# Three exchanges in the order in which a linear-attention and feed-forward kernel issues its loads

## The chip, the core and the metric

The kernel runs on one core of a Trainium2 chip. The core has a matrix engine (TensorE, PE in the profile; its weight loads are shown as PEld), two elementwise engines (VectorE, DVE; ScalarE, ACT), a general one (GpSimd, POOL) and SyncE (SP), which here does nothing but issue transfers between the chip's main memory and the core's SBUF. Each engine works through its own list of instructions in order and waits on semaphores for the others. The metric is the device time of one execution in microseconds; lower is better. A comparison goes by the median of several executions.

## What is computed

Causal linear attention with a decay per head, over 4 batches, 8 heads, 768 positions and head size 64, and behind it a feed-forward layer with a leaky ReLU. Inputs are q, k, v, the decay `lam`, and the weights `w_in` (512 x 2048) and `w_out` (2048 x 512). The weights arrive as float64.

```python
for b in range(nb):                                   # blocks of 64 positions
    qb, kb, vb = (q[:, :, sl], k[:, :, sl], v[:, :, sl])
    intra = np.einsum('bhic,bhjc->bhij', qb, kb) * Dmask[None]
    intra = np.einsum('bhij,bhjd->bhid', intra, vb)
    inter = np.einsum('bhid,bhde->bhie', qb * lam_pow[None], kv_state)
    out[:, :, sl] = intra + inter
    kb_dec = kb * rev_pow[None]
    kv_state = lam_block[None, :, None, None] * kv_state + np.einsum('bhsd,bhse->bhde', kb_dec, vb)
...
x = attn_out.transpose(0, 2, 1, 3).reshape(B * S, H * D)   # 3072 x 512
h = x @ w_in
g = np.maximum(0.01 * h, h)
return g @ w_out
```

## The kernel before

**Chunks.** The attention goes through 24 chunks of 128 positions (6 per batch), all 8 heads at once. For chunk c, `load_kq` loads k and q (two transfers each, L476) and `load_v` loads v (one transfer, L538). `transposes` turns k and q on TensorE (L560) into PSUM; copies on ACT or DVE (L541) bring them back as kT and qT, and L608 makes a scaled copy of qT. `scores` has two products: `kv`, the state update from k and v, and `go`, the scores from kT and qT (both L420). `outputs` has three: `own` (scores times v), and the halves `inter(0)` and `inter(1)` of the product of q with the states (L420). Between the two halves stands a tiny copy from PSUM, `seen_po` (L692), on ACT or DVE; `inter(1)` waits for it. L708, L716 and L734 then write the chunk's result as three parts xh, xl, xm, which keep float32 accuracy in the product with the weights. Up to chunk 7, q is loaded like k; from chunk 8 on it comes in small pieces of 32x8x32 (L523).

**Weights.** `w_in` is taken in 8 blocks p of 256 columns, each in two halves h. `to_float32` loads one half as float64 into one of three buffers raw0, raw1, raw2 (two transfers of 256 KB, L798), and builds a float32 of it: three steps on ACT (L810, L812, L814) and two on DVE (L816, L817). `parts` splits the block into a head wh (L823), wm (L826) and wl (L828). `up` multiplies a group of four chunks with one block (L864), and `down` the result with `w_out` (L930), with TensorE alone at work for the last half of the time.

**Order.** `Plan` holds every step as an operation with a number, an engine, what it reads and what it writes. The list `ORDER` (L266) fixes the order of the first 1296 entries by hand: pairs of an operation number and an engine, "DMA" being SP. An entry with a negative number stands for idle products that keep TensorE busy. What comes behind the list is ordered by a planner's costs. Each engine gets its operations in the order of the list; only the order among entries of the same engine matters. Semaphore waits follow from what each operation reads and writes. SP's line in the list is one queue: a transfer whose buffer is not free yet holds up every transfer behind it.

**The entries that the change touches,** all on SP:

| entry | what it loads | who needs it |
|---|---|---|
| 95 | first half of w_in block 1, into raw1, two transfers | steps 97 (L812), 96 (L810), 98 (L814) on ACT, 99 and 100 on DVE, then wh1 (107, L823 on ACT) |
| 50 | q of chunk 2, two transfers | transpose 53 (L560) |
| 74 | v of chunk 3, one transfer | `kv` of chunk 3 (81, L420) |
| 111 | q of chunk 4, two transfers, into the buffer of q of chunk 2 | transpose 114 (L560) |
| 355 | second half of w_in block 7, into raw2, two transfers | steps 356 (L810), 357 (L812), 358 (L814) on ACT, then wh7 |
| 275 | one small piece of the q of chunks 8 and 9 | DVE transposes (L532) |
| 303 | v of chunk 8, one transfer | `kv` of chunk 8 (310, L420) |

On ACT the order around them is 102 (L810), 103 (L812), 97 (L812), 104 (L814), 96 (L810), 98 (L814), 44 (L692, chunk 1), 54 (L541), 46 (L708), 107 (L823); operations 101 to 106 belong to the other half of block 1, which is loaded into raw0 just ahead of entry 95. Later it is 356, 357, 358, 309 (L692, chunk 7), 313 (L708). On DVE it is 106 (L817, second half), 55 (L541), 99 (L816), 100 (L817, first half).

## Time and profile before

| | |
|---|---|
| median of 3 executions | 607.43 us (606.27 to 608.04) |
| profiled execution | 606.49 us, of which 604.7 us from the first to the last instruction |
| TensorE | busy 595.9 us, 99% of the span, granted clock 1.0 |
| DVE, ACT, POOL | 49%, 35%, 12% |
| read from and written to main memory | 68.69 and 35.65 MB, 173 GB/s over the span |

Times in the profile are microseconds from the start of the span. A line names the kernel's line (L798), the engine, the operation, and what it writes and reads by the program's tile names; in brackets stands the idle time of the engine ahead of it and what ended that. SPq is SP's queue: there, start and length are those of the issue, not of the transfer. When a transfer lands is shown by the view of transfers, as the time from issue to landing. The tile `att` holds all of the attention's buffers, so k, q and v of most chunks are written to it; chunks 2 and 3 use `gs` and `raw` for some of theirs. Every product of 64x64 or 128x128 tiles in float32 shows as one or two matmuls.

### The profile page before, as it was taken

To read this page: it belongs to the slowest core of one execution; us is meant where nothing else is said; L and a number is where in the kernel's file an instruction comes from. 1 tells how busy PE (TensorE), PEld (TensorE's weight loads), DVE (VectorE), ACT (ScalarE), POOL (GpSimd) and SP (SyncE) were. 2 spreads that over 40 slices of the span, in tenths; PEclk is the share of its full clock that TensorE was granted. 3 is DMA by queue.
4 is the path that set the end of the run, shared out by engine and by line. 5 is a ranking of instruction groups with operands and counts; after the bars stand their busy time and mean duration, and the time that the engine had idled before them with its cause. 6 is when DMAs were issued, how large, how long until landed. Compare 5 with 4: busy or idle time off the path is not lost.

```text
span 604.7 us, 12740 instructions
## 1 busy us (share of the span) xinstructions
PE 595.9 (99%) x5362; PEld 492.0 (81%) x5362; DVE 294.4 (49%) x410; ACT 209.2 (35%) x323; POOL 70.0 (12%) x84
## 2 busy tenths in 40 slices
PE   8899999999999999999999999999999999999997
PEld 5788888888888888887888888888888888888886
DVE  6798754450554434244167755354353543534430
ACT  4686651212433433435334421222312313214111
POOL 2311232241322031140000000000000000000000
PEclk9999999999999999999999999999999999999999
DMA  9998887597788788664975823433333333423201
GB/s 208 226 266 224 224 241 199 88 258 188 214 227 210 224 241 232 183 203 181 327 258 184 302 105 128 151 99 134 116 116 128 118 126 122 125 102 124 85 1 69
DMA packets 150249, 105.18 MB, mean 174 GB/s; under 512 B 126128, under 2 KB 126896, under 8 KB 150192
## 3 DMA queue, kind: packets, MB, share of 16 engines
q1 hardware_dynamic: 148848, 104.03, 58.6%
q8 instruction: 42, 0.69, 0.5%
q10 hardware_dynamic: 1344, 0.33, 0.2%
q14 instruction: 15, 0.12, 0.1%
HBM read 68.69 MB, written 35.65 MB: 173 GB/s over the span
## 4 chain that ended last, share of the span: by engine, by line
PE 95%; DMA 2%; SPq 1%; issue 0%; ACT 0%; DVE 0%; DVEq 0%; ACTq 0%
PE b L864 32%; PE b L930 16%; PE pt L864 11%; PE psc L930 11%; PE po L930 11%; PE pt L930 5%; PE po L420 4%; PE psc L420 3%; DMA att<-in_v_dram 2%; DMA att<-in_q_dram 1%; PE b L560 0%; PE po L560 0%; SPq L798 0%; PE b L420 0%; PE b L359 0%
## 5 line engine op out<-in xcount | busy, mean ns | idle before, releaser
L912 DVE SCALAR_TENSOR_TENSOR xl<-att,xh 128x1024 fp32r<-128x1024 f32 x48 | 58.7, 1223 | 125.8 <-ACT xh L911 125.8
L911 ACT ACTIVATE xh<-att 128x1024 fp32r<-128x1024 f32 x48 | 50.9, 1061 | 147.5 <-PE po L930 73.0
L864 PE MATMUL b<-xl,wl 128*128 128x512 f32 (+1 forms) x292 | 77.1, 388 | 0.0
L864 PE MATMUL b<-xh,wh 128*128 128x512 f32 (+1 forms) x292 | 76.5, 389 | 0.6 <-ACT wh L823 0.6
L864 PE MATMUL b<-xm,wm 128*128 128x512 f32 (+1 forms) x292 | 76.0, 390 | 0.0
L891 ACT ACTIVATE gs<-b 128x512 f32<-128x512 f32 x72 | 42.1, 597 | 96.3 <-PE b L864 87.1
L864 PEld LDWEIGHTS b<-xh,wh 128*128 128x128 f32 x292 | 53.9, 188 | 11.8 <-ACT wh L823 0.7
L864 PEld LDWEIGHTS b<-xl,wl 128*128 128x128 f32 x292 | 54.1, 188 | 11.2
L864 PEld LDWEIGHTS b<-xm,wm 128*128 128x128 f32 x292 | 53.8, 188 | 11.2
L914 DVE SCALAR_TENSOR_TENSOR xm<-xl,xh 128x1024 fp32r<-128x1024 f32 x48 | 58.8, 1226 | 4.7
L930 PE MATMUL b<-wh,xh 128*128 128x512 f32 x144 | 56.0, 389 | 0.0
L930 PE MATMUL b<-wl,xl 128*128 128x512 f32 x144 | 56.0, 389 | 0.0
L930 PE MATMUL b<-wm,xm 128*128 128x512 f32 x144 | 56.0, 389 | 0.0
L663 POOL TENSOR_TENSOR att<-att 128x256 f32<-128x256 f32 x40 | 27.8, 694 | 113.9 <-DVE att L660 66.2
L930 PE MATMUL psc<-wm,xm 128*128 128x512 f32 (+1 forms) x100 | 38.2, 387 | 0.0
L930 PE MATMUL po<-wm,xm 128*128 128x512 f32 (+1 forms) x100 | 37.9, 384 | 0.0
L930 PE MATMUL psc<-wh,xh 128*128 128x512 f32 x96 | 37.3, 389 | 0.0
L930 PE MATMUL psc<-wl,xl 128*128 128x512 f32 x96 | 37.3, 389 | 0.0
L930 PE MATMUL po<-wh,xh 128*128 128x512 f32 x96 | 37.3, 389 | 0.0
L930 PE MATMUL po<-wl,xl 128*128 128x512 f32 x96 | 37.3, 389 | 0.0
L420 PEld LDWEIGHTS po<-att 64*64 64x64 f32 x1408 | 27.0, 134 | 10.5 <-issue 7.8
L420 PE MATMUL po<-att 64*64 64x64 f32 x1408 | 33.0, 222 | 1.7 <-issue 0.9
(106 smaller groups left out, 860.5 us busy)
## 6 DMA issues: line engine op xcount, KB each, us to landing
att<-g SPq DMA_DIRECT2D x48, 512.0 KB, 3.4
g<-gs SPq DMA_DIRECT2D x47, 512.0 KB, 3.6
raw<-in_moe_w_in_dram SPq DMA_DIRECT2D x32, 256.0 KB, 4.3
raw<-in_moe_w_out_dram SPq DMA_DIRECT2D x16, 512.0 KB, 4.6
out_dram<-gs SPq DMA_DIRECT2D x23, 256.0 KB, 2.1
att<-in_v_dram SPq DMA_DIRECT2D x22, 256.0 KB, 3.8
att<-in_k_dram SPq DMA_DIRECT2D x43, 128.0 KB, 3.9
wo<-w SPq DMA_DIRECT2D x8, 512.0 KB, 4.0
```

What stands on the lines that cost most here:

```text
L420: nc.tensor.matmul(dst[HALF[cols]], lhsT=lhsT[HALF[rows]], rhs=rhs[HALF[rows]], start=start, stop=True, skip_group_check=True)
L663: add("POOL", 0.62, lambda new=new, j=j: behind(("s", j), nc.gpsimd.tensor_tensor(state[(j + 1) % 4], new, _bc(lam_c, 2, D), op=ALU.mult)) ...
L864: nc.tensor.matmul(dst, lhsT=w[z][:, kk * 2 * P + f * P:kk * 2 * P + (f + 1) * P], rhs=x[z][:, kk, toks], start=start and kk == 0, stop=kk ...
L891: add("ACT", ns, lambda b=b, r=r: nc.scalar.activation(out=r(), in_=b(), func=AF.Prelu, bias=0.0, scale=1.0, alpha=0.01), [kb], [kg], rank ...
L911: add("ACT", 1.05, lambda: nc.scalar.activation(out=h, in_=graw[j], func=AF.Copy, bias=0.0, scale=NEAR), reads, wr("h"))
L912: add("DVE", 1.215, lambda: nc.vector.scalar_tensor_tensor(l, graw[j], 1.0, h.bitcast(F32), op0=ALU.mult, op1=ALU.subtract), reads + [f"rh ...
L914: add("DVE", 1.215, lambda: nc.vector.scalar_tensor_tensor(m, l.bitcast(F32), -S, h.bitcast(F32), op0=ALU.mult, op1=ALU.add), [f"rh{j}", f ...
L930: nc.tensor.matmul(to[:, cols], lhsT=ring[j][z][:, f * T + tb * P:f * T + (tb + 1) * P], rhs=W[pp][z][:, f * d_model:(f + 1) * d_model][:, ...
```

## The change

Three places of `ORDER` are changed. Only entries of SP change their order among themselves; the other entries are moved along in the text of the list, but keep their order on their engines.

1. q of chunk 2 (50) is issued ahead of the first half of w_in block 1 (95), which was ahead of it.
2. q of chunk 4 (111) is issued ahead of v of chunk 3 (74).
3. v of chunk 8 (303) is issued where the second half of w_in block 7 (355) was, ahead of one small q piece (275), and 355 where v of chunk 8 was, behind that piece.

```diff
-    ... (101, "DMA"), (95, "DMA"), (50, "DMA"), (20, "PE"), (49, "DMA"), (72, "DMA"), ...
+    ... (101, "DMA"), (50, "DMA"), (95, "DMA"), (20, "PE"), (49, "DMA"), (72, "DMA"), ...
...
-    ... (98, "ACT"), (44, "ACT"), (74, "DMA"), (41, "POOL"), ... (57, "DVE"), (111, "DMA"), (58, "PE"), ...
+    ... (98, "ACT"), (44, "ACT"), (111, "DMA"), (74, "DMA"), (41, "POOL"), ... (57, "DVE"), (58, "PE"), ...
...
-    ... (304, "DMA"), (355, "DMA"), (288, "ACT"), (275, "DMA"), (207, "POOL"), ... (293, "DVE"), (303, "DMA"), ...
+    ... (304, "DMA"), (303, "DMA"), (275, "DMA"), (355, "DMA"), (288, "ACT"), (207, "POOL"), ... (293, "DVE"), ...
```

## The prediction

> **What bounds the kernel now.** I read the page's first two lines, then the stretches from 30 us on, then TensorE's waits. The columns of the first fence are engine, busy time, share and instructions.

> ```profile
> span 604.7 us, 12740 instructions
> PE 595.9 (99%) x5362; PEld 492.0 (81%) x5362; DVE 294.4 (49%) x410; ACT 209.2 (35%) x323; POOL 70.0 (12%) x84
> ```

> By stretches (from:to, its length, busy time of PE, PEld, DVE, ACT, POOL, granted clock, DMA share, GB/s):

> ```profile
> 30.00:67.00 37.00, 36.98 (x613) 31.61 (x615) 31.42 (x49) 26.20 (x48) 7.88 (x11) 1.00 0.87 234
> 75.00:300.00 225.00, 225.00 (x2741) 185.91 (x2740) 92.28 (x176) 81.77 (x146) 52.01 (x56) 1.00 0.77 213
> 300.00:595.00 295.00, 295.00 (x1303) 244.35 (x1302) 140.93 (x122) 77.89 (x93) 0.00 (x0) 1.00 0.39 133
> ```

> From 75 to 595 us TensorE is never idle. So whatever the change wins or loses must be won or lost before 75 us, and from there it goes to the end one for one: nothing behind it can absorb a delay, and nothing can lengthen a gain. What there is to win stands in TensorE's waits (who waited for whom, total us, times, longest):

> ```profile
> PE po L420 <- issue: 0.9, 1, 0.9
> PE b L560 <- DMA att<-in_q_dram: 0.6, 1, 0.6
> PE b L864 <- ACT wh L823: 0.6, 1, 0.6
> PE psc L420 <- DMA att<-in_v_dram: 0.5, 1, 0.5
> ```

> The second is the transpose of q of chunk 4, the fourth the state product of chunk 8, which needs v8. The chain that ended last passes through the same two loads (start, length from issue to landing):

> ```profile
> 20.64 5.37 DMA att<-in_q_dram
> 64.17 3.54 DMA att<-in_v_dram
> ```

> q4's second half lands at 26.01, v8 at 67.71. Both would land earlier. The third wait, for the head wh1 of w_in block 1, is what the first exchange could lengthen.

> **The change part by part.** Nothing is added or removed. Every engine but SP keeps its order, and on SP the same loads are issued, so what is costed is when each load lands and who stands in line behind it.

> *Exchange 1, q2 ahead of the first half of w_in block 1 (entry 95).* SP's issues (start, length, operation):

> ```profile
> 7.12 2.49 SPq L798 DMA_DIRECT2D raw<-in_moe_w_in_dram  x4
> 9.19 0.43 SPq L798 DMA_DIRECT2D raw<-in_moe_w_in_dram  x1
> 9.66 0.98 SPq L476 DMA_DIRECT2D att<-in_q_dram  x2
> 10.14 0.51 SPq L476 DMA_DIRECT2D att<-in_q_dram  x1
> ```

> Landings of the pieces issued at 9.19, 9.66 and 10.14, in that order (the last column is us from issue):

> ```profile
> raw<-in_moe_w_in_dram SPq DMA_DIRECT2D x1, 256.0 KB, 4.4
> ...
> att<-in_q_dram SPq DMA_DIRECT2D x1, 128.0 KB, 5.8
> ...
> att<-in_q_dram SPq DMA_DIRECT2D x1, 128.0 KB, 5.7
> ```

> The load of w lands at 9.19 + 4.4 = 13.6, q2's halves at 15.4 and 15.8. The loads of this queue land in the order of issue, so in the new order w comes last of the four, and between 14.4 and 15.8: at the least 0.4 us for each q2 half (the distance of their own landings) after 13.6, at the most where the four together end now. I take 15.8: same queue, same bytes, same stretch of time. That is 2.2 us later. Now the line behind it. ACT and DVE (start, length, operation):

> ```profile
> 13.66 0.79 ACT L812 ACTIVATE low<-raw 128x512 uint16<-128x512 uint32 x1
> ...
> 14.30 0.76 ACT L814 ACTIVATE low<-raw 128x512 f16<-128x512 f32 x1
> 14.93 0.65 ACT L810 ACTIVATE w<-raw 128x512 f32<-128x512 f32 x1
> 15.47 0.79 ACT L814 ACTIVATE low<-raw 128x512 f16<-128x512 f32 x1
> 17.03 0.16 ACT L692 COPY att<-po 128x2 f32<-128x2 f32 x1 [0.77 <-PE po L420]
> ...
> 18.61 1.05 ACT L823 CAST wh<-w 128x1024 fp32r<-128x1024 f32 x1
> ...
> 15.32 0.68 DVE L817 CUSTOM_DVE_ANT_0 w<-w,low 128x1024 uint16<-128x1024 uint16 x1
> 16.61 0.69 DVE L541 COPY att<-b 128x512 f32<-128x512 f32 x1 [0.60 <-PE b L560]
> ...
> 17.77 0.69 DVE L817 CUSTOM_DVE_ANT_0 w<-w,low 128x1024 uint16<-128x1024 uint16 x1
> ```

> The L812 at 13.66 reads this load, and it stands in ACT's line ahead of an L814 that works on the other half (already landed), ahead of two more steps on w, and ahead of the L692 copy that lets TensorE go on with chunk 1. All of them move by 2.2: the L814 of 14.30 ends at 15.06 + 2.2 = 17.3; L692 starts at about 18.4 instead of 17.03. On DVE the first L817 needs that L814 and starts 0.26 behind it, at 17.5; the L541 copy behind it at 18.15; the second L817, 1.16 after the copy, at 19.3, and ends at 20.0. The cast of wh1 starts 0.15 behind it as now: 20.15, ends 21.2, against 19.66. The other way to it, L692, then TensorE's second half of chunk 1, then the copy xh, then the cast, gives about 19.85 and is not the last. So the product on wh1 is 1.5 us late. On the way to the transpose of q4 at 24.9 I let TensorE make good 0.2 (an estimate: waits for loads that do not move, each below the 0.15 us at which the view begins): +1.3.

> What q2 gains is worth nothing: its transpose starts right behind the 0.9 us of "issue" in the waits, in which TensorE waited for no load, and that stays. If that stall went, q2's landing would be the next to hold it, now early.

> *Exchange 2, q4 ahead of v3.*

> ```profile
> 19.48 0.43 SPq L538 DMA_DIRECT2D gs<-in_v_dram  x1
> 20.01 1.45 SPq L476 DMA_DIRECT2D att<-in_q_dram  x2
> ```

> q4 goes to the place of v3 and lands before the 26.01 of now, whatever v3 takes. TensorE comes to its transpose at 24.9 + 1.3 = 26.2, so the 0.6 wait is gone, and 0.1 more before its second half: -0.7. v3 takes the last place of the three and lands by 26.0 (where they end now); its first user starts at 26.9 now and at 27.5 then. q4's issue also waits for its buffer, until the transposes of q2 are done, and those are over by 16.6; v3 and v8 wait for no buffer, so nothing is held on SP by the new order. Balance of the two exchanges: 1.3 - 0.7 = +0.6. Without exchange 1 the second alone would give about -0.7.

> *Exchange 3, v8 ahead of the second half of w_in block 7 (entry 355).* Its two pieces go behind v8 and behind one small q piece:

> ```profile
> 61.46 2.19 SPq L798 DMA_DIRECT2D raw<-in_moe_w_in_dram  x2
> 61.96 1.69 SPq L798 DMA_DIRECT2D raw<-in_moe_w_in_dram  x1
> 63.70 0.42 SPq L523 DMA_DIRECT2D att<-in_q_dram  x1
> 64.17 0.45 SPq L538 DMA_DIRECT2D att<-in_v_dram  x1
> ```

> Landing of the piece issued at 61.96:

> ```profile
> raw<-in_moe_w_in_dram SPq DMA_DIRECT2D x1, 256.0 KB, 4.3
> ```

> So w is complete at 66.3 and v8 at 67.7. ACT and TensorE behind them:

> ```profile
> 66.37 0.70 ACT L810 ACTIVATE w<-raw 128x512 f32<-128x512 f32 x1 [2.77 <-DMA raw<-in_moe_w_in_dram]
> ...
> 68.24 0.14 ACT L692 COPY att<-po 128x2 f32<-128x2 f32 x1
> ...
> 67.84 1.16 PE L420 MATMUL psc<-att 64*64 64x64 f32 x64 [0.53 <-DMA att<-in_v_dram]
> 68.79 0.44 PE L420 MATMUL po<-att 64*64 64x64 f32 x16
> ```

> With v8 early TensorE's 67.84 becomes 67.3, and its 68.79 (the second half of chunk 7) 68.3. But that one needs the L692 copy, and the copy stands in ACT's line behind three steps on w: it starts 1.87 after the L810, and TensorE can follow 0.2 later. The new landing of w is between 66.3 (v8 fits into the pauses) and 67.7 (the end of the three loads now). I take 67.3, 66.3 plus v8's 256 KB at the 0.4 us that 128 KB of q took above, and a little: the L810 at 67.4, the copy at 69.25, TensorE at 69.45 instead of 68.79: +0.65. The ends are 66.3: 68.45, -0.35, and 67.7: 69.85, +1.05. The wait is not removed, it goes from v8 to w, by way of ACT. The stream here is started by TensorE's own progress, so the +0.6 of before is added. What w itself is for (head wh7) is used by TensorE only near 81 us and does not matter.

> *The fetch of instructions.* The landings above are not even: w at 13.6, then q2 only at 15.4. In that stretch the program's instructions are also fetched. The page's row for it, and the count in the one microsecond from 12.5 us (queue, kind, number, MB, share):

> ```profile
> q8 instruction: 42, 0.69, 0.5%
> ...
> q8 instruction: 1, 0.02, 7.0%
> ```

> I count the gap as part of the stretch, and so whichever load is last pays it. [...]

> **The sum.** 1.3 - 0.7 + 0.65 = +1.25 us. The profiled execution took 606.49 us, which becomes 607.7; it lies 0.9 under the median of the three runs, 607.43, so for the median: 608.6 us, 0.2% slower. About 0.3%, 1.8 us, is what a measurement of this kernel can tell from no change, so this counts as no change.

> **The rivals.**
> - *The delayed w is hidden.* w lands at the lower ends, 14.4 and 66.3. Then ACT loses 0.8 in exchange 1, of which the pause of 0.77 ahead of L692 covers all, exchange 2 gives -0.7, exchange 3 -0.35: about -1.0, 606.4 us. For it: the pause in ACT's line. Against: q2's own landings, which the loads behind w needed until 15.8.
> - *Faster beyond the bound.* All three named load waits go and the wh1 wait too: 0.7 + 0.5 + 0.6 = 1.8, 605.6 us. It needs wh1 to come earlier, and nothing in the change makes its loads earlier.
> - *Slower beyond the bound (the other side).* The place is ACT's L812 at 13.66. Every 0.1 us by which the w load lands after 15.8 goes to the end, since exchange 2 has no more wait to give. From a landing of 16.4 on the sum passes 1.8 us; at 17.2, if the gap of 1.8 us between 13.6 and 15.4 hits two loads rather than one, the time is 610.0 us. For it: 256 KB pieces instead of 128 KB ones then lie in the stretch of the gap. Against: total bytes are the same.

> **How the numbers follow.** The forecast, +0.3 to +1.8, has 0.57; the hidden case, -1.8 to +0.3, 0.18; slower beyond the bound 0.21; faster beyond it 0.04. So faster 0.04, same 0.75, slower 0.21. The range leaves out a tenth at each side: from just above the hidden case's 606.4, 606.5, to the slow rival's 610.1. The forecast's own range is 607.7 to 609.2.

> **What would show it.** Right: ACT's L812 on the second raw buffer starts near 15.9, the wait of TensorE for wh1 (L823) grows from 0.6 to about 2 us together with a wait behind L692, the waits for q4 and v8 are gone from the list, and a wait of about 1.1 us at the L420 po near 69.5 for ACT's L692 is new. Wrong: no such wait near 69 us (w7 landed in time), or L812 near 14.5, or an idle TensorE beyond 75 us, where I take it to have none.

## The result, and the profile after

The changed kernel takes 608.60 us (median of 17 executions, 607.27 to 613.65), the kernel before 606.91 us beside it (17 executions, 606.08 to 608.91). The ratio on record goes by all of these executions and is 1.0042, 95% interval 1.0028 to 1.0056; the two medians alone give 1.0028. In a second comparison it was 608.54 against 606.65 us, ratio 1.0030 (1.0015 to 1.0046). So the number on record was met to the tenth, but the effect was larger: the forecast was +1.2 us, and between the medians +1.7 and +1.9 us were measured. Both intervals exclude no change, so the kernel is slower; whether by more than the 0.3% that the prediction took as the bound of no change, they do not settle. How +1.2 and +1.7 come about also differs, and that is what the experiments are about.

The profiled execution took 607.27 us (span 605.5), the fastest of the 17. TensorE's waits in it, and the stretches behind 75 us (columns as in the prediction):

```profile
PE po L420 <- ACT att L692: 3.2, 2, 1.7
PE b L359 <- POOL att L362: 1.4, 1, 1.4
PE b L864 <- ACT wh L823: 0.7, 1, 0.7
PE po L420 <- issue: 0.4, 1, 0.4
```

```profile
75.00:300.00 225.00, 225.00 (x2742) 186.03 (x2741) 92.90 (x175) 82.42 (x147) 52.24 (x56) 1.00 0.78 213
300.00:595.00 295.00, 295.00 (x1303) 244.29 (x1302) 141.69 (x123) 77.90 (x93) 0.00 (x0) 1.00 0.40 133
```

The waits for q of chunk 4 and for v8 are gone, and two waits for ScalarE's copy L692 stand in their place, 1.5 and 1.7 us. Behind 75 us TensorE is still never idle, so a delay at 75 us is the delay at the end. The first pause, in the timeline of ACT and then of PE:

```profile
16.28 0.78 ACT L812 ACTIVATE low<-raw 128x512 uint16<-128x512 uint32 x1 [2.49 <-DMA raw<-in_moe_w_in_dram]
...
18.72 0.14 ACT L692 COPY att<-po 128x2 f32<-128x2 f32 x1
...
20.20 1.04 ACT L823 CAST wh<-w 128x1024 fp32r<-128x1024 f32 x1
```

```profile
18.93 0.46 PE L420 MATMUL po<-att 64*64 64x64 f32 x16 [1.50 <-ACT att L692]
...
21.30 0.73 PE L864 MATMUL b<-xh,wh 128*128 128x256 f32 x4 [0.70 <-ACT wh L823]
...
25.40 0.64 PE L864 MATMUL b<-xh,wh 128*128 128x256 f32 x4
25.87 0.60 PE L560 MATMUL b<-att 128*128 128x128 f32 x4
```

The second transfer of entry 95 lands at 16.26 (before: 13.6), the L812 that reads it starts at once, and the copy L692 behind it lets TensorE go on at 18.93. The last row is the transpose of q of chunk 4: no bracket, so no wait. The second pause, SP's issues ahead of it, then ACT, then PE:

```profile
61.20 0.50 SPq L538 DMA_DIRECT2D att<-in_v_dram  x1
61.75 1.74 SPq L523 DMA_DIRECT2D att<-in_q_dram  x1
63.59 0.87 SPq L798 DMA_DIRECT2D raw<-in_moe_w_in_dram  x2
```

```profile
67.68 0.66 ACT L810 ACTIVATE w<-raw 128x512 f32<-128x512 f32 x1 [4.29 <-DMA raw<-in_moe_w_in_dram]
...
69.50 0.13 ACT L692 COPY att<-po 128x2 f32<-128x2 f32 x1
```

```profile
66.92 1.11 PE L420 MATMUL psc<-att 64*64 64x64 f32 x64
69.70 0.46 PE L420 MATMUL po<-att 64*64 64x64 f32 x16 [1.67 <-ACT att L692]
```

v8 lands at 65.31 and the state product starts at 66.92 without a wait. Entry 355 is complete at 67.66, and through three steps and the copy it holds TensorE until 69.70, which was 68.79.

### The profile page after: what moved, and what is told of

It is laid out like the page before. It is cut to its first block, busy times and chain, and to the rows that moved or that the text cites. A ratio compares the mean times of both kernels' runs of the same rounds, so it can differ in the third digit from the quotient of the medians.

```text
span 605.5 us, 12741 instructions
## 1 busy us (share of the span) xinstructions
PE 595.0 (98%) x5362; PEld 491.6 (81%) x5362; DVE 295.0 (49%) x410; ACT 209.4 (35%) x323; POOL 70.0 (12%) x84
## 4 chain that ended last, share of the span: by engine, by line
PE 94%; SPq 2%; DMA 2%; ACT 1%; DVE 1%; issue 0%; DVEq 0%
PE b L864 32%; PE b L930 16%; PE pt L864 11%; PE psc L930 11%; PE po L930 11%; PE pt L930 5%; PE po L420 4%; PE psc L420 3%; DMA raw<-in_moe_w_in_dram 2%; SPq L476 1%; SPq L798 0%; PE po L560 0%; SPq L523 0%; SPq L538 0%; PE b L560 0%
## 5 line engine op out<-in xcount | busy, mean ns | idle before, releaser
L864 PE MATMUL b<-xh,wh 128*128 128x512 f32 (+1 forms) x292 | 76.5, 389 | 0.7 <-ACT wh L823 0.7
L864 PE MATMUL b<-xl,wl 128*128 128x512 f32 (+1 forms) x292 | 77.1, 388 | 0.0
L864 PE MATMUL b<-xm,wm 128*128 128x512 f32 (+1 forms) x292 | 75.9, 390 | 0.0
L891 ACT ACTIVATE gs<-b 128x512 f32<-128x512 f32 x72 | 42.0, 595 | 94.2 <-PE b L864 81.4
L864 PEld LDWEIGHTS b<-xh,wh 128*128 128x128 f32 x292 | 53.8, 188 | 12.0 <-ACT wh L823 0.8
L864 PEld LDWEIGHTS b<-xl,wl 128*128 128x128 f32 x292 | 54.1, 188 | 11.2
L864 PEld LDWEIGHTS b<-xm,wm 128*128 128x128 f32 x292 | 53.8, 188 | 11.2
L663 POOL TENSOR_TENSOR att<-att 128x256 f32<-128x256 f32 x40 | 27.5, 686 | 110.2 <-DVE att L660 61.3
L420 PEld LDWEIGHTS po<-att 64*64 64x64 f32 x1408 | 26.9, 134 | 13.2 <-issue 7.0
L420 PE MATMUL po<-att 64*64 64x64 f32 x1408 | 33.0, 222 | 4.3 <-ACT att L692 3.2
## 6 DMA issues: line engine op xcount, KB each, us to landing
raw<-in_moe_w_in_dram SPq DMA_DIRECT2D x32, 256.0 KB, 4.3
out_dram<-gs SPq DMA_DIRECT2D x23, 256.0 KB, 2.1
att<-in_v_dram SPq DMA_DIRECT2D x22, 256.0 KB, 4.2
att<-in_k_dram SPq DMA_DIRECT2D x43, 128.0 KB, 3.9
```

The costliest lines, as they stand in the source:

```text
L420: nc.tensor.matmul(dst[HALF[cols]], lhsT=lhsT[HALF[rows]], rhs=rhs[HALF[rows]], start=start, stop=True, skip_group_check=True)
L663: add("POOL", 0.62, lambda new=new, j=j: behind(("s", j), nc.gpsimd.tensor_tensor(state[(j + 1) % 4], new, _bc(lam_c, 2, D), op=ALU.mult)) ...
L864: nc.tensor.matmul(dst, lhsT=w[z][:, kk * 2 * P + f * P:kk * 2 * P + (f + 1) * P], rhs=x[z][:, kk, toks], start=start and kk == 0, stop=kk ...
L891: add("ACT", ns, lambda b=b, r=r: nc.scalar.activation(out=r(), in_=b(), func=AF.Prelu, bias=0.0, scale=1.0, alpha=0.01), [kb], [kg], rank ...
```

## The experiments

What is called TensorE's place is the start of the same matmul in a kernel less its start in the profile of the kernel before. For the changed kernel it is +1.45 at the first pause, +1.1 at 25.4 us, -0.2 at 41 us, -0.9 at 66.9 (v8 is there), +0.9 at 69.7 and +0.75 at the end. The place rests on one profile of the kernel before. Four other profiles have the order of before up to 60 us (exchange 3 alone, twice, and its two variants below); at 41 us their places are -0.5, +0.8, -0.5 and +0.1, so that a difference of some 0.5 us between two profiles says little by itself. The recorded expectations call entry 95 the second half of w's first tile, and entry 355 the second half of its eighth.

### Each exchange alone

```diff
-    ... (101, "DMA"), (95, "DMA"), (50, "DMA"), ...
+    ... (101, "DMA"), (50, "DMA"), (95, "DMA"), ...
```

> Exchange 1 alone: q2 ahead of the first half of w_in block 1. Theory 'line' (a late w load holds ACT's line, the L692 copy and wh1 with it): TensorE waits about 1.5 us for L692 near 19 us and the product on wh1 starts near 21.3 us instead of 19.7. TensorE then reaches the transpose of q4 late and no longer waits 0.6 us for it, so that by 60 us most of the 1.6 us is made good: 0 to +0.7 us in the profiled execution. Rival 'it adds up': +1.6 us at 20 us stays to the end. Rival 'clock': the pause of TensorE costs it granted clock in some executions (the mean granted clock was below 1.000 in most of the executions of the changed kernel); then the median is 1 to 2 us over that of before although a profile at clock 1.000 shows under 0.7, and the executions below clock 1.000 are the slow ones.

```diff
-    ... (44, "ACT"), (74, "DMA"), ... (57, "DVE"), (111, "DMA"), ...
+    ... (44, "ACT"), (111, "DMA"), (74, "DMA"), ... (57, "DVE"), ...
```

> Exchange 2 alone: q4 ahead of v3. Theory: q4 lands 1.3 to 2.5 us earlier, the 0.6 us wait of TensorE for it goes from the list, v3 is in time; TensorE is 0.7 to 1.2 us earlier from 27 us on, and the time is 0.7 to 1.2 us lower. Rival 'v3 late': v3 now lands near 26 us and its user comes at 25.8 us, so that the wait changes its name, and the gain is below 0.3 us.

```diff
-    ... (304, "DMA"), (355, "DMA"), (288, "ACT"), (275, "DMA"), ... (303, "DMA"), ...
+    ... (304, "DMA"), (303, "DMA"), (288, "ACT"), (275, "DMA"), (355, "DMA"), ...
```

> Exchange 3 alone: v8 ahead of the second half of w_in block 7. Theory 'line': the wait of 0.5 us for v8 goes, and a wait of 1.2 to 1.7 us for the L692 copy comes in its place near 69.7 us; TensorE is 0.9 to 1.1 us later from 70 us on, and the time is higher by as much. Rival 'hidden': the ACT steps on w are off the path, the wait for v8 simply goes, -0.5 us. Rival 'clock': more than 1.1 us in the median, with a granted clock below 1.000 in the slow executions.

| kernel | median, us | before, us | ratio (95%) |
|---|---|---|---|
| exchange 1 alone | 608.17 (606.95 to 609.71) | 607.23 | 1.0010 (0.9995 to 1.0025) |
| exchange 2 alone | 607.50 (606.16 to 611.49) | 607.23 | 1.0005 (0.9988 to 1.0023) |
| exchange 3 alone | 608.96 (607.29 to 613.24) | 607.23 | 1.0033 (1.0013 to 1.0052) |

Exchange 3 is the one that costs, about 2.0 us by its ratio; the other two can't be told from nothing. The profile of exchange 1 ends at +0.6, inside what its theory gave, but most of the delay was not made good by 60 us, where the place is +1.2. Its rival 'clock' is not borne out: the median is 0.9 us up, and the three fastest of its 12 executions are at clock 0.997.

Exchange 2 by itself brings no gain, and its theory fell. TensorE runs through the transpose of q4 (first row), and two later loads, a v and the k of chunk 8, then hold it:

```profile
25.41 0.60 PE L560 MATMUL b<-att 128*128 128x128 f32 x4
...
41.74 1.09 PE L420 MATMUL psc<-att 64*64 64x64 f32 x46 [0.45 <-DMA att<-in_v_dram]
...
58.86 0.41 PE L560 MATMUL po<-att 128*128 128x128 f32 x2 [0.33 <-DMA att<-in_k_dram]
```

But TensorE runs through that transpose without exchange 2 as well. These are the same rows in the two profiles of exchange 3 alone, which have the old order there:

```profile
25.35 0.60 PE L560 MATMUL b<-att 128*128 128x128 f32 x4
...
24.78 0.60 PE L560 MATMUL b<-att 128*128 128x128 f32 x4
```

The second half of q4 lands at 24.03 and 24.72 us in these two, and at 26.01 in the profile of before. Of the five profiles that have neither exchange 1 nor 2, before alone shows the wait in full, one shows about 0.4 us of it inside the group, and three show none. So there was mostly no wait for exchange 2 to take.

Exchange 3 alone shows the wait of the changed kernel, in the same place, as its theory 'line' said; its profile ends at +0.8, while the median is 1.7 us up, and the three executions at clock 0.997 or below (611.2 to 613.2 us) are its three slowest:

```profile
67.26 1.17 PE L420 MATMUL psc<-att 64*64 64x64 f32 x64
69.84 0.46 PE L420 MATMUL po<-att 64*64 64x64 f32 x16 [1.42 <-ACT att L692]
```

### Is it the transfer, or the line on ScalarE behind it? (exchange 3)

First both L692 and L708 of chunk 7 ahead of the three steps on entry 355 (on DVE, entry 359, which works on the same half, also goes behind 353), then L692 alone:

```diff
-    ... (356, "ACT"), ... (357, "ACT"), ... (358, "ACT"), ... (309, "ACT"), (359, "DVE"), ... (313, "ACT"), ...
+    ... (309, "ACT"), ... (313, "ACT"), (356, "ACT"), (357, "ACT"), (358, "ACT"), (359, "DVE"), ...
```

> Exchange 3 alone, and on ACT the three steps on the second half of w_in block 7 (L810, L812, L814) stand behind the L692 copy and the L708 of chunk 7 instead of ahead of them; the loads are those of the run with exchange 3 alone. Theory 'line': neither the wait for v8 nor that for L692 is left, TensorE is 0.4 to 0.6 us earlier than before from 70 us on, and the time is lower by as much. Rival 'the transfers': if the loss of exchange 3 came from the transfers themselves (the fuller queue, or q pieces landing later), it stays at about +1 us.

```diff
-    ... (356, "ACT"), ... (357, "ACT"), ... (358, "ACT"), ... (309, "ACT"), (359, "DVE"), ... (313, "ACT"), ...
+    ... (309, "ACT"), (356, "ACT"), (357, "ACT"), (358, "ACT"), (359, "DVE"), ... (313, "ACT"), ...
```

> Exchange 3 alone, with only the copy L692 of chunk 7 moved ahead of ScalarE's steps on the second half of w's eighth tile; the other steps stand in their order behind it. Theory (exchange 3 costs what L692 behind the w steps costs): no wait for L692 at 69 us, TensorE within -0.5 to +0.3 us of the kernel before at 70 to 76 us, no execution with a mean clock of 0.997 or less, 607.0 to 607.8 median. Rival (the w steps are late for the next reader as well, as when L708 too was put ahead): a wait of 0.5 to 1 us at 70 to 73 us for ScalarE's L708 or L891, 607.8 to 608.3.

With both ahead: 607.84 us, ratio 1.0013 (0.9995 to 1.0030). With L692 alone: 607.70 against 606.30 us, ratio 1.0015 (1.0000 to 1.0031). PE of the first:

```profile
69.04 0.41 PE L420 MATMUL po<-att 64*64 64x64 f32 x16
...
72.45 1.88 PE L864 MATMUL b<-xh,wh 128*128 128x512 f32 x7 [0.95 <-ACT gs L891]
```

and of the second, with ACT:

```profile
68.47 0.41 PE L420 MATMUL po<-att 64*64 64x64 f32 x16
...
71.91 1.20 PE L864 MATMUL pt<-xh,wh 128*128 128x512 f32 x4 [1.88 <-ACT xh L708]
```

```profile
69.47 0.66 ACT L810 ACTIVATE w<-raw 128x512 f32<-128x512 f32 x1 [1.83 <-DMA raw<-in_moe_w_in_dram]
...
71.28 0.58 ACT L708 ACTIVATE xh<-po 128x512 fp32r<-128x512 f32 x1
```

In both the wait at L692 is gone, so it was ACT's line and not v8 or the state product. But both theories fell, that of the first kernel (0.4 to 0.6 us earlier than before) and that of the second (this is all exchange 3 costs): the steps on the late w then stand ahead of whatever comes next, L708 (1.88 us) or L891 (0.95 us). The bill of the late load is passed along ACT's line. By the ratios about half of it is saved, though the intervals overlap that of exchange 3. By the traces the saving is 0.5 us: between 66 and 76 us TensorE loses 0.9 and 2.2 us in the two profiles of exchange 3 alone, 0.5 with both ahead, and 1.7 with L692 alone ahead, where w is as late as in the second of those two. The rival of the second kernel had the mechanism right, but not the sizes: its wait of 0.5 to 1 us was 1.88, and its 607.8 to 608.3 us were not reached.

### The same question for exchange 1

Exchange 1 alone, with the three steps on entry 95 behind L692 and L541 of ACT:

```diff
-    ... (97, "ACT"), (104, "ACT"), (96, "ACT"), ... (98, "ACT"), (44, "ACT"), ... (54, "ACT"), ...
+    ... (104, "ACT"), ... (44, "ACT"), ... (54, "ACT"), (97, "ACT"), (96, "ACT"), (98, "ACT"), ...
```

> Exchange 1 alone, with ScalarE's steps on the second half of w's first tile (both L812 and L814 of it) moved behind the copy at L692 of chunk 1, so that only the transfer is late and nothing on ScalarE stands behind it. Theory (in exchange 1 the lateness has two bills, the copy L692 and then wh1, and they overlap): no wait for L692 at 17 to 19 us, but the wait for wh1 at 19 to 22 us grows from 0.7 to about 1.5 to 2.2 us, and TensorE is as late behind it as in exchange 1 alone (+1 to +2 us at 22 us). Rival (the line on ScalarE is the whole of it, as in exchange 3): wait for wh1 stays at 0.7 or below, TensorE within 0.3 us of the kernel before at 22 us.

607.93 against 606.30 us, ratio 1.0024 (1.0011 to 1.0037).

```profile
18.58 0.46 PE L420 MATMUL po<-att 64*64 64x64 f32 x16
...
23.03 0.74 PE L864 MATMUL b<-xh,wh 128*128 128x256 f32 x4 [2.78 <-ACT wh L823]
```

The wait for L692 is gone and the one for wh1 has grown from 0.7 to 2.8 us, more than expected. It does not separate the load from the line as I meant it to. Entry 95 was complete at 14.69 us here, against 16.05 to 16.47 in the six other profiles with exchange 1, and L812 started only at 19.22, behind L541. So this wait for wh1 is the price of three steps that stand behind the copies, not of a late load. Whether the waits for L692 and wh1 in exchange 1 cover each other stays open.

### Where does exchange 2's gain go?

Exchange 2 alone, and the load of k of chunk 8 two places earlier:

```diff
-    ... (208, "DMA"), ... (280, "DMA"), ... (278, "DMA"), ... (283, "DMA"), ...
+    ... (208, "DMA"), (283, "DMA"), ... (280, "DMA"), ... (278, "DMA"), ...
```

> Exchange 2 alone, with the load of k of chunk 8 moved two places ahead, before two other loads that are wanted later. Theory (exchange 2 takes a wait of 0.7 to 1.1 us away at 26 us, and loses it again at 58 us, where k of chunk 8 lands just in time for a TensorE that comes earlier): no wait at 58 us, TensorE 0.4 to 0.9 us earlier than before from 26 us to beyond 60 us, and 606.3 to 606.9 median, ratio 0.9985 to 0.9995, unless the next load is late in turn. Rival (no gain from exchange 2 reaches 58 us, or the gain goes at a third place): TensorE within 0.3 us of before at 60 to 70 us, 607.2 to 607.6.

607.11 against 606.30 us, ratio 1.0006 (0.9995 to 1.0018), so the theory fell. The wait at 58 us is gone, yet no gain is left; a k and a v take it at a third place:

```profile
39.67 0.71 PE L560 MATMUL po<-att 128*128 128x128 f32 x4 [0.51 <-DMA att<-in_k_dram]
...
41.54 1.09 PE L420 MATMUL psc<-att 64*64 64x64 f32 x46 [0.30 <-DMA att<-in_v_dram]
...
57.89 0.60 PE L560 MATMUL po<-att 128*128 128x128 f32 x4
```

TensorE's place is -0.95 at 38 us, -0.3 where the k lets it go on, and +0.1 behind the v: in this profile the loads at 40 us, and not q4, decide where TensorE stands. The four profiles with the old order are at -0.3 to -1.1 behind q4 too, so most of what looks like a gain at 26 us comes from the long wait in the one profile of before. Of the rival, the place holds (+0.1 at 60 us), and the time lies 0.1 us below what it said.

### Is the rest the clock?

In all 83 executions of the kernel before for which the record lists it, the mean granted clock is 0.999 or 1.000. Of 29 executions of the changed kernel 20 lie at 0.997 or below. Three profiles have a stretch at half clock inside the span, each 3.41 us long (their times stand in the last section), and each of these executions is listed at 0.997. One such stretch takes 0.28% off the mean over the span, so 0.997 is one of them and 0.994, by the same sum, would be two. To take these stretches away I let TensorE multiply dummy data in the two pauses:

```diff
-    ... (41, "POOL"), (45, "PE"), ... (406, "DMA"), (312, "PE"), ...
+    ... (41, "POOL"), (-10, "PE"), (45, "PE"), ... (406, "DMA"), (-10, "PE"), (312, "PE"), ...
```

> All three exchanges, and products on dummy data (ten of 128x512 and ten of 128x128) put on TensorE just ahead of the two products that wait for ScalarE's L692 at 17 to 19 and at 68 to 70 us, so that TensorE works through the two pauses without doing anything useful. Theory of the clock (the pauses bring a stretch of half clock in most executions of the changed kernel, and that is the larger part of its 1.7 us): TensorE's useful products stand where they stand in the changed kernel within some 0.5 us, but the mean granted clock is 0.999 or 1.000 in nearly all executions, where 12 of 17 of the changed kernel lie at 0.997 or below; median 607.5 to 608.1, ratio to the kernel before 1.001 to 1.002. Rival (the clock's lower mean has to do with something other than the pauses, the chip or the transfers): clocks spread as for the changed kernel, median 608.5 or more. Rival (the filler is in the way): clock at 1.000 and the wait for L692 replaced by more than 0.5 us of later products, 608.5 or more.

The filler (L359 is the line of such idle products) is smaller than its expectation says: the trace has four matmuls of it in each pause, two of 128x512 and two of 128x128, together 1.25 and 1.35 us. The clock was at 0.997 in 2 of 12 executions, against 20 of 29 unfilled. So the pauses do cause the half clock. But the time is 608.16 against 606.30 us, ratio 1.0034 (1.0019 to 1.0048), no better than unfilled within the intervals: the gain that the theory of the clock forecast did not come. The filler left the pause's end where the late w puts it:

```profile
67.93 1.35 PE L359 MATMUL pt<-att 128*128 128x512 f32 x4
70.17 0.46 PE L420 MATMUL po<-att 64*64 64x64 f32 x16 [0.90 <-ACT att L692]
```

The clock's share stays open all the same. In the two comparisons of the changed kernel the 8 executions at 0.999 or above take 608.0 us in the mean and the 19 below them 609.8, but a longer pause brings both a later TensorE and the half clock, so these 1.8 us are not the clock's alone. The 10 filled executions at 0.999 or above take 608.5 us, no less than the 8.

### More profiles of the same two kernels

The profile shows +0.75 at the end, the median +1.7, and that profile was the fastest execution. So the changed kernel and exchange 3 alone were profiled again, unchanged. (A "look" in the expectations is a profile.)

> The changed kernel once more, for a second profile beside the one of 607.27 us, which was the fastest of its 17 executions. What has the median execution 1.3 us more? Theory A (lateness of w scatters): the same two waits for ScalarE's L692, one or both longer than 1.5 and 1.7 us, because the second half of w's first tile lands after 15.4 us or that of the eighth after 67.7 us. Theory B (clock): a stretch of half clock between 17 and 26 us or 66 and 76 us, with TensorE's products in it twice as long. Theory C (later meetings): waits of 0.5 us or more after 76 us for k, q or v, that the profile of 607.27 us does not have. Time 607.3 to 611 us.

> As the second look: theories A, B and C as there. If the two looks lose their time in different places, none of the three alone is the rest.

> As the second look: theories A, B and C as there. If it too loses its time elsewhere, the rest is a scatter of several meetings.

> Exchange 3 alone once more; its median (608.97 us) lies 1.7 us above its first profile (607.29 us). Theory A: the second half of w's eighth tile lands later than 67.7 us and the wait for L692 near 69 us is 2 us or more in place of 1.4. Theory B: half clock between 66 and 76 us. Theory C: waits of 0.5 us or more after 76 us for k, q or v. 607.3 to 611 us.

| profile | time, us | issue that is stretched | entry 355 lands | TensorE's place at 41 us, behind the L692 wait, at the end |
|---|---|---|---|---|
| changed, first | 607.27 | q | 67.66 | -0.21, +0.91, +0.75 |
| changed, second | 607.30 | q | 67.82 | +0.05, +1.09, +0.79 |
| changed, third | 610.60 | v8 | 69.23 | -0.13, +2.48, +4.11 |
| changed, fourth | 606.81 | entry 355, first transfer | 67.30 | -0.23, +0.56, +0.31 |
| exchange 3, first | 607.29 | entry 355, first transfer | 67.79 | -0.47, +1.05, +0.79 |
| exchange 3, second | 609.25 | v8 | 69.75 | +0.80, +2.99, +2.76 |

Only two of the four new profiles are slow, and none lies near the medians of 608.5 and 609.0 us; the fourth of the changed kernel is even faster than the range on record. In the two slow ones theory A holds, and in the third of the changed kernel theory B on top of it. C does not: behind 76 us none of the six has a wait that the view shows, and the place moves by 0.3 us at most. SP's issues and the wait in the third profile of the changed kernel, to be held against those of its first above:

```profile
61.29 2.15 SPq L538 DMA_DIRECT2D att<-in_v_dram  x1
63.49 0.58 SPq L523 DMA_DIRECT2D att<-in_q_dram  x1
64.17 0.87 SPq L798 DMA_DIRECT2D raw<-in_moe_w_in_dram  x2
```

```profile
71.27 0.46 PE L420 MATMUL po<-att 64*64 64x64 f32 x16 [2.70 <-ACT att L692]
```

An issue takes some 0.5 us (v8's 0.50 in the first profile, the q piece's 0.58 in the third); one of them is stretched to between 1.4 and 2.2 us in every profile of the two kernels and of the kernel before. In the trace one block of instructions of 16 KiB (42 of them make up the page's 0.69 MB) is fetched at just that time (third profile: from 61.49 to 63.03), and in each of these seven profiles the stretched issue is the one under way when the fetch ends, and ends 0.38 to 0.54 us after it. Where that is v8's issue, nothing of entry 355 is queued, and the transfers run dry. Stretches of the first profile, then of the third (the last two columns are DMA share and GB/s):

```profile
62.30:63.30 1.00, 1.00 (x6) 0.82 (x5) 0.56 (x1) 1.00 (x2) 0.83 (x2) 1.00 0.82 184
63.30:64.30 1.00, 1.00 (x7) 0.80 (x6) 0.46 (x2) 0.10 (x1) 0.40 (x1) 1.00 0.82 174
```

```profile
62.30:63.30 1.00, 1.00 (x6) 0.82 (x5) 0.65 (x2) 1.00 (x3) 1.00 (x2) 1.00 0.46 100
63.30:64.30 1.00, 1.00 (x6) 0.84 (x5) 0.56 (x2) 0.19 (x1) 0.40 (x2) 1.00 0.14 29
```

Counted from SP's issue of the k ahead of the three, entry 355 is complete after 5.6 to 6.1 us in the five profiles without exchange 3, after 7.1 to 7.5 us in five with it where another issue than v8's is stretched, and after 7.9 to 8.9 us in the four where it is v8's (among them the filled pauses and L692 alone ahead). So the exchange delays w by about 1.5 us in the one case and 2.7 us in the other (differences of the means). That the fetch is the cause is read from its coincidence in every profile; a kernel in which the fetch was moved on purpose was not tried. By itself its time varies, near 13 us too, and the landings there go with it. In 11 profiles a fetch begins at 12.5 to 13.1 us, and the two halves of q2 and the two transfers of entry 95 have all landed by 15.8 to 16.5. In three (exchange 2 alone, the first of exchange 3 alone, and exchange 1 with the steps behind the copies) it begins at 13.8 to 14.1, and they have all landed by 14.7 to 14.8.

## Why the prediction was right or wrong

- **All is decided before 75 us.** Right in every profile, to within about 0.4 us.
- **Exchange 1, the line behind w.** Right to within 0.5 us: L812 at 16.28 (said 15.9), L692 at 18.72 (18.4), the cast at 20.20 (20.15), the product on wh1 at 21.30, +1.6 (+1.5), +1.1 at 25.4 (+1.3). The landing, 16.26, lay beyond the upper end of 15.8, so that the cast came out to the tenth owes something to luck; the wait for L692 and that for wh1 make 2.2 us together (about 2).
- **The fetch of instructions.** The gap in the landings does fall on the load that is last, as counted, in six of the seven profiles with exchange 1; in the seventh, with the later fetch, entry 95 is complete at 14.69, near the lower end. SP's issues are longer where a block is fetched: in the profile after, blocks are fetched from 12.54 to 13.73 and from 16.76 to 17.70 us; four issues from 10.76 take 3.49 us and one from 16.60 takes 1.53, where v8's at 61.20 takes 0.50.
- **Exchange 2, -0.7.** The step that failed is "the 0.6 wait is gone": it takes the wait of one execution for a wait of the kernel, and of four other profiles with the old order three do not have it and one has 0.4 us of it. In the one profile it was also mis-sized: the place falls by 1.15 there. The wait was in two parts, and I took the second for 0.1. Its row in the timeline of before:

```profile
25.55 0.95 PE L560 MATMUL b<-att 128*128 128x128 f32 x4 [0.64 <-DMA att<-in_q_dram]
```

  Four such transposes take 0.60 us where nothing stops them; here they take 0.95, so 0.35 us more were lost inside the group, where no bracket shows it. That the second exchange alone "would give about -0.7" was wrong in the time: 0.3 us slower, with an interval of about 1 us to either side. The balance of the first two exchanges, forecast as +0.6, is -0.1 at 41 us (mean of four profiles of the changed kernel); profiles with the old order alone lie from -0.5 to +0.8 there, so the two can't be told apart.
- **Exchange 3, +0.65 (between -0.35 and +1.05).** The mechanism was right: v8's wait goes, and w by way of ACT and L692 takes its place; the rival "the delayed w is hidden" is out. The size was wrong. Behind the wait TensorE is at +0.91, +1.09, +2.48 and +0.56, and was at about -0.1 ahead of the exchange: +1.4 in the mean. The step that failed is the upper end of the landing, "67.7 (the end of the three loads now)": I took the end of the group as fixed and only dealt out the places in it. The end moves, since the stretched issue of SP may now stand ahead of w, and then the queue runs dry (29 GB/s from 63.3 to 64.3 us in the third profile): entry 355 was complete at 67.30 to 67.82 in the four profiles where another issue is stretched, and at 69.23 and 69.75 in the two where it is v8's.
- **The sum.** +0.6 and +0.65 were forecast; -0.1, +1.4 and, in the one profile of the changed kernel with a stretch of half clock, 1.6 for the clock (below) were measured. The wrong terms nearly cancel. That the point on record was met exactly is luck; it also hangs on the median it was put on, 607.43 of three executions, where larger sets of the kernel before have medians of 606.30 to 607.23.
- **The chances.** The case of slower by over 0.3% had 0.21, for a w in exchange 1 that lands later still. By the ratios, 1.0042 and 1.0030, the change lies at or above that bound, with intervals that reach below it. What put it there is a w that lands later than the given end, but in exchange 3, where I had given the same mechanism a closed range.

## What to carry to other kernels

Two loads exchanged in a full queue need not simply trade their landings: here the one put back landed up to 2 us later than the group's end suggested (69.75 against 67.7) when the issuing engine itself was held up ahead of it (2.12 us for v8's issue), so its price needs the spread of several profiles and not the times of one. The same holds for a wait that is to be removed: see first whether a second profile of the kernel has it. Before a late load is moved ahead, look what stands behind the one that is put back on its consumer's line; here three steps on a weight that nobody needed for 12 us held up a copy of 0.14 us that TensorE needed at once, and moving that copy forward only handed the bill to the next in line. And see whether the later loads that TensorE waits for leave a gain at one wait standing; with exchange 2 and k earlier, waits of 0.51 and 0.30 us for a k and a v at 40 us took it.

## What the runs showed of the hardware

```profile
69.30:72.60 3.30, 1.33 (x20) 1.13 (x21) 1.63 (x4) 2.70 (x6) 0.00 (x0) 1.00 0.54 175
72.70:76.10 3.40, 3.40 (x9) 2.67 (x8) 3.40 (x7) 2.94 (x5) 0.00 (x0) 0.50 0.85 233
...
72.70:76.10 3.40, 3.40 (x16) 2.81 (x15) 3.40 (x6) 3.11 (x4) 0.00 (x0) 1.00 0.88 187
```

TensorE is busy again since 71.27, yet from 72.69 it gets half clock and does 9 matmuls in 3.4 us, where the first profile does 16 in the same stretch; TensorE's place goes from +2.5 to +4.1, and stays there. In exchange 1 alone the half clock comes from 21.77 to 25.18 us, behind a grid window with 1.94 us of busy TensorE, and the place goes from +1.8 to +2.5 in it. In the grid windows up to 77 us of all 14 profiles half clock followed windows with 0.78, 1.42 and 1.94 us of busy TensorE; windows with 1.71 and 1.87 went without, and the kernels that have no window below 2.3 us (before, exchange 2 with and without k earlier, L692 and L708 ahead, pauses filled) show 0.997 in 3 of 130 executions. So if the busy time of a window is what counts, the limit lies near half a window (an estimate from these five windows), and it is not sharp in the busy time as the profile models it. The length of a pause does not decide it alone: single pauses of 2.70 us (third profile of the changed kernel) and 2.78 us (steps behind the copies), and one of 1.36 us followed by one of 0.70 (exchange 1 alone), had half clock behind them, and one of 2.43 us in the second profile of exchange 3 alone had none.
